# The 16-point stage of an H3 convolution: kernel spectrum without rearranged copies, five VectorE products

## The chip, the cores and the metric

The kernel runs on one core of a Trainium2 chip. The metric is device time in microseconds (us), from one launch to its end; the time before is the median of three runs. A core has a matrix engine (TensorE; in the profile PE for its matmuls and PEld for the loads of their stationary operand), a vector engine (VectorE, DVE), an engine for copies and functions (ScalarE, ACT), GpSimd (POOL) and SyncE (SP), which issues transfers. Matmuls write to PSUM, which has 8 banks of 2 KB in each of 128 partitions; everything else lies in SBUF.

## The reference

The model has four layers, A, B, A, B, on a sequence of S = 2048 rows of D = 576 channels, each one a residual around a layer norm:

```python
def _A_ref(x, ...):                     # Fourier mixing as matmuls
    a = einsum("bsd,ed->bse", x, dft_hid_re); b = einsum("bsd,ed->bse", x, dft_hid_im)
    return einsum("ts,bse->bte", dft_seq_re, a) - einsum("ts,bse->bte", dft_seq_im, b)

def _B_ref(q, k, v, shift_k, ssm_k, ssm_D):
    kv = (short causal convolution of k with shift_k) * v
    y = irfft(rfft(pad(kv)) * rfft(pad(ssm_k)))[:S]     # long causal convolution, per channel
    return q * (y + kv * ssm_D)

x = x + A(layernorm(x)); x = x + B(layernorm(x), k, v, ...)
x = x + A(layernorm(x)); x = x + B(layernorm(x), k, v, ...)
```

k, v and the two kernels are inputs, so the long convolution y is the same in both B layers and does not depend on x. It is computed once.

## The kernel before, in words

Layer A is done as two sets of float32 matmuls: the sequence transform (128x512 tiles, in four blocks of output rows, `layer` at L291) and behind it the hidden transform (`hidden`, L267, 27 matmuls of 128x288 for each of two halves of a row group). Every float32 operand is split in a rounded high part and a remainder, and each product is three matmuls (high by high, high by low, low by high). The split is one ScalarE copy and one VectorE subtraction (`split`, L90, lines L91 and L92 of the profile).

The long convolution is a Fourier transform in two factors, 128 by 16, written as a generator (`branch`, L338) that the loop over the first layer A advances piece by piece, so that its matmuls stand between those of the layer. It has three stages: 128-point products (tile f1r), then the 16-point stage (MID), then 128-point products of the inverse (i2). The loop sets the order by costs that it adds up: from its step MID_FROM = 47 to I2_END = 111 it counts what part of the layer has been issued and draws from the generator until the branch has had the same part (L746 to L754). The numbers that the generator yields are these costs.

The 16-point stage has 64 groups (mids): two halves of the channels by 32 groups of four frequencies, 288 channels wide. For each group the generator issues, in this order:

- `mid_inverse` (L515) of an earlier group: three matmuls, a ScalarE copy out of PSUM and a store;
- `mid_kernel` (L493): three matmuls give the spectrum of the convolution kernel in PSUM (pk), with real parts in partitions 0 to 63 (lo) and imaginary parts in 64 to 127 (hi). ScalarE copies pk into half 0 of an SBUF tile kk, and then makes three more copies of 64 partitions within kk, so that half 0 holds the real parts twice and half 1 the imaginary parts with the two signs that the complex product needs;
- `mid_round` (L510) of the group before: the split of its product (line L485 on ScalarE, L491 on VectorE);
- `mid_signal` (L501): three matmuls give the spectrum of the signal in PSUM (px); VectorE makes the complex product out of a product of 128 partitions (L504), two of 64 (L505 and L506) and a sum (L507). The result lies in kk's half 0;
- the split of the operand that is needed two groups later (`split_feed`, again L485 and L491, 576 wide) and the next load.

The ScalarE instructions of the stage are recorded at L485, a helper (`act`) that also chains each one behind the one before it. The matmuls are all at L74. The PSUM tiles of the stage (name bk) are taken in turn from three banks, which the hidden transform uses too; the sequence transform has five banks of its own (s and rm). A bank is free again when the copy or the last product that reads it is done.

Of the kernel before, what the change touches and what calls it, by code (L numbers as in the profile page):

```python
# [12 lines left out]
AF = mybir.ActivationFunctionType  # L13
OP = mybir.AluOpType
# [7 lines left out]
HD = D // 2  # L22
# [42 lines left out]
def fnet_h3_kernel(ctx: ExitStack, tc: tile.TileContext, x, c_mat, w_re, w_im, k_pad, v, shift_k,  # L65
                   ssm_k, ssm_d, f1c, i2c, midc, out):
    nc = tc.nc
# [68 lines left out]
    def two(v):  # L136
        return v.rearrange("p (a n) -> p a n", a=2)
# [200 lines left out]
    def branch():  # L338
# [132 lines left out]
        lo, hi = slice(0, 64), slice(64, 128)  # L471

        def mid_half(df, o):
            ps = bank()
            mm(ps[:, :HD], mc[:, 0, :], df[0][:, o:o + HD], True, False)
            mm(ps[:, :HD], mc[:, 0, :], df[1][:, o:o + HD], False, False)
            mm(ps[:, :HD], mc[:, 1, :], df[0][:, o:o + HD], False, True)
            return ps
# [3 lines left out]
        def act(*args, **kw):  # L482
            if last_act:
                with tc.issue_after(last_act[-1]):
                    last_act.append(nc.scalar.activation(*args, **kw).ins)  # L485
            else:
                last_act.append(nc.scalar.activation(*args, **kw).ins)
# [5 lines left out]
        def mid_kernel(df):  # L493
            pk, kk = mid_half(df, HD), two(ring["kk"]())
            act(kk[:, 0, :], pk[:, :HD], AF.Copy)
            act(kk[lo, 1, :], kk[hi, 0, :], AF.Copy)
            act(kk[hi, 1, :], kk[hi, 0, :], AF.Copy, scale=-1.0)
            act(kk[hi, 0, :], kk[lo, 0, :], AF.Copy)
            return kk

        def mid_signal(df, kk):  # L501
            px = mid_half(df, 0)
            p1, p2 = kk[:, 0, :], ring["p2"]()
            nc.vector.tensor_tensor(p1, px[:, :HD], p1, OP.mult)  # L504
            nc.vector.tensor_tensor(p2[lo], px[hi, :HD], kk[hi, 1, :], OP.mult)  # L505
            nc.vector.tensor_tensor(p2[hi], px[lo, :HD], kk[lo, 1, :], OP.mult)  # L506
            nc.vector.tensor_tensor(p1, p1, p2, OP.add)  # L507
            return p1

# [62 lines left out]
        for i, (kind, hf, q) in enumerate(feeds):  # L572
            df = halves.pop(i)
            if kind:
                i2_products(hf, q, fcs.pop(used), df)
                load_fc(used + ahead)
                used += 1
            else:
                if len(yfs) == MID_LAG:
                    mid_inverse(*yfs.pop(0))  # L580
                    yield 0.4
                kk = mid_kernel(df)
                if product is not None:
                    yfs.append((*product[:2], mid_round(product[2])))
                yield 1.6
                product = hf, q, mid_signal(df, kk)
# [517 lines left out]
```

## Time and profile before

| | before |
|---|---|
| time, median of three runs | 1202.64 us (1201.62 to 1203.9) |
| the profiled execution's own time | 1203.45 us |
| its span, first to last instruction | 1201.7 us |
| mean granted TensorE clock | 0.998 |
| TensorE matmuls busy | 1181.4 us (98%) |
| weight loads busy | 1026.7 us (85%) |
| VectorE busy | 839.9 us (70%) |
| ScalarE busy | 666.0 us (55%) |
| the 16-point stage's first and last product on VectorE | 222.4 and 550.0 us |

Busy time is the union of an engine's instruction records; the matmuls' ends are modelled, so that a busy TensorE may still lose time between two matmuls. In a table of stretches of time a row has the stretch and its length, then for PE, PEld, DVE, ACT and POOL the busy time with the number of instructions, then the granted clock, the share of the transfer engines and their GB/s; where it is asked for one tile or line, it has the busy time of those instructions alone. In a group of instructions stand line, engine, operation, output<-inputs, shapes and count, then busy time and the mean of one in ns, then the idle time before them. "Idle before" in a row is the idle time of that engine right before the instruction, with the instruction that ended it. In a list of waits the columns are the total, the number of waits and the longest. In a timeline they are the start, the busy time, the engine, the line, the operation, output<-inputs, the number of merged instructions, and in brackets the idle time before.

### The profile page before, as it was taken

What the parts mean: (1) busy time and instruction counts of PE and PEld (TensorE: products, weight loads), DVE (VectorE), ACT (ScalarE), POOL (GpSimd) and SP (SyncE); (2) the same over time, 40 slices, a digit from 0 to 9 for tenths busy, and PEclk for the clock granted to TensorE, in tenths of its full rate; (3) what the DMA queues carried; (4) which work ended last, traced back from release to release, by engine and by line L of the source; (5) the groups of instructions that cost most, each with busy time, mean ns of one, the idle gap of its engine ahead of it and who ended that gap; (6) DMA issues with size and microseconds to landing.
All of it is one profiled execution on the core that took longest, in us unless ns stands there. A gap on an engine that the chain in (4) does not pass through costs nothing.

```text
span 1201.7 us, 18251 instructions
## 1 busy us (share of the span) xinstructions
PE 1181.4 (98%) x6320; PEld 1026.7 (85%) x6320; DVE 839.9 (70%) x1498; ACT 666.0 (55%) x1335; POOL 75.3 (6%) x116
## 2 busy tenths in 40 slices
PE   7999999999999999999999999999999999999997
PEld 6888888988888888888988898888888888789997
DVE  7889983679777677675447766865776777674764
ACT  7865665679877768675435666534444445450210
POOL 2210000000000000001101121000000000001111
PEclk9999999999999999999999999999999999999999
DMA  9879898546756767648967686872772786795621
GB/s 355 273 242 310 282 296 262 177 133 182 217 183 194 212 178 207 194 143 247 308 202 237 221 257 204 278 259 71 225 274 71 216 283 213 270 339 155 218 92 40
DMA packets 146110, 261.95 MB, mean 218 GB/s; under 512 B 15841, under 2 KB 44769, under 8 KB 146018
## 3 DMA queue, kind: packets, MB, share of 16 engines
q1 hardware_dynamic: 102674, 205.58, 53.5%
q10 hardware_dynamic: 36432, 42.63, 10.2%
q0 software_dynamic: 6912, 12.59, 3.9%
q8 instruction: 49, 0.80, 0.3%
q14 instruction: 43, 0.35, 0.1%
HBM read 194.09 MB, written 66.65 MB: 217 GB/s over the span
## 4 chain that ended last, share of the span: by engine, by line
PE 84%; DVE 5%; ACT 4%; DMA 4%; issue 2%; POOL 1%; SPq 0%; ACTq 0%; POOLq 0%; DVEq 0%
PE s L74 46%; PE bk L74 33%; PE rm L74 5%; ACT flts L485 1%; DMA flts<-in_c_mat 1%; DVE mats L189 1%; DMA t<-ud 1%; DVE mats L92 1%; DVE f1f L386 1%; DMA t<-flts 1%; ACT mid L485 1%; ACT mats L91 1%; POOL flts L615 0%; DVE f1f L381 0%; DMA flts<-in_ssm_k 0%
## 5 line engine op out<-in xcount | busy, mean ns | idle before, releaser
L74 PE MATMUL s<-mats 128*128 128x512 f32 x2088 | 531.4, 392 | 1.3 <-DVE u L92 0.8
L74 PEld LDWEIGHTS s<-mats 128*128 128x128 f32 x2088 | 381.7, 188 | 71.9 <-DVE u L92 1.7
L92 DVE TENSOR_TENSOR mats<-flts,mats 128x512 fp32r<-128x512 f32 x206 | 141.1, 687 | 60.9 <-ACT mats L91 57.8
L91 ACT ACTIVATE mats<-flts 128x512 fp32r<-128x512 f32 x206 | 128.6, 628 | 81.8 <-PE bk L74 33.8
L74 PE MATMUL bk<-mid 128*128 128x288 f32 x768 | 131.2, 300 | 1.7 <-ACT flts L485 0.9
L74 PEld LDWEIGHTS bk<-mid 128*128 128x128 f32 x768 | 114.3, 188 | 21.3 <-ACT flts L485 8.4
L491 DVE TENSOR_TENSOR mid<-flts,mid 128x576 fp32r<-128x576 f32 (+1 forms) x160 | 101.9, 637 | 33.6 <-ACT mid L485 28.0
L74 PE MATMUL bk<-w,u 128*128 128x288 f32 x864 | 120.8, 296 | 0.4 <-DVE w L232 0.4
L74 PEld LDWEIGHTS bk<-w,u 128*128 128x128 f32 x864 | 117.3, 188 | 4.1 <-ACT flts L485 1.3
L485 ACT ACTIVATE flts<-bk 128x288 f32<-128x288 f32 x160 | 62.0, 405 | 86.8 <-PE bk L74 73.9
L74 PE MATMUL rm<-mats 128*128 128x512 f32 x304 | 94.9, 391 | 0.0
L485 ACT ACTIVATE mid<-flts 128x576 fp32r<-128x576 f32 (+1 forms) x159 | 86.7, 582 | 7.3 <-DMA flts<-t 3.3
L485 ACT ACTIVATE flts<-flts 64x288 f32<-64x288 f32 x192 | 85.0, 443 | 5.9 <-ACT flts L485 0.4
L431 ACT ACTIVATE flts<-bk 128x288 f32<-128x288 f32 x128 | 49.2, 409 | 47.1 <-PE bk L74 40.0
L74 PE MATMUL bk<-f1r 128*128 128x288 f32 x384 | 64.9, 301 | 7.2 <-ACT f1r L91 7.2
L74 PEld LDWEIGHTS bk<-f1r 128*128 128x128 f32 x384 | 59.8, 192 | 14.2 <-ACT f1r L91 7.6
L74 PE MATMUL bk<-mats 128*128 128x288 f32 (+1 forms) x376 | 67.8, 317 | 0.0
L74 PEld LDWEIGHTS rm<-mats 128*128 128x128 f32 x304 | 56.9, 188 | 12.1 <-DVE flts L264 0.3
L74 PE MATMUL s<-t,mats 128*128 128x512 f32 x264 | 65.5, 390 | 1.6 <-DVE t L92 1.6
L278 DVE TENSOR_TENSOR flts<-flts,bk 128x288 f32<-128x288 f32 x48 | 21.8, 453 | 63.2 <-PE bk L74 61.0
L175 POOL TENSOR_TENSOR flts<-flts 128x1 f32<-128x1 f32 x35 | 29.6, 846 | 526.0 <-DVE flts L174 522.6
L74 PEld LDWEIGHTS s<-t,mats 128*128 128x128 f32 x264 | 49.5, 188 | 12.2 <-DVE t L92 2.0
(143 smaller groups left out, 1500.7 us busy)
## 6 DMA issues: line engine op xcount, KB each, us to landing
flts<-in_c_mat SPq DMA_DIRECT2D x148, 256.0 KB, 3.7
ph<-in_c_mat SPq DMA_DIRECT2D x54, 512.0 KB, 4.4
t<-flts ACTq DMA_DIRECT2D x64, 288.0 KB, 4.5
flts<-t SPq DMA_DIRECT2D x64, 288.0 KB, 2.9
flts<-in_c_mat SPq DMA_DIRECT2D x30, 512.0 KB, 5.0
vd<-flts ACTq DMA_DIRECT2D x64, 144.0 KB, 2.3
flts<-vd SPq DMA_DIRECT2D x32, 288.0 KB, 4.9
mid<-in_i2c POOLq DMA_DIRECT2D x32, 256.0 KB, 5.6
```

Of the source, the lines that this page charges most:

```text
L74: nc.tensor.matmul(ps, lhsT, rhs, start=first, stop=last, skip_group_check=more)
L91: a = nc.scalar.activation(h, src, AF.Copy).ins
L92: return a, nc.vector.tensor_tensor(l, src, h.bitcast(F32), OP.subtract).ins
L175: pows.append(nc.gpsimd.tensor_tensor(rs, ve, mhalf, OP.pow).ins)
L189: made.append(nc.vector.tensor_tensor(t[:, D + REM:], y[:, :NC * P], h[:, :NC * P], OP.subtract).ins)
L278: added[:] = [nc.vector.tensor_tensor(r[:, cs], r[:, cs], ps[:, :HD], OP.add).ins]
L386: nc.vector.tensor_tensor(rp, rp, out_t, OP.add)
L431: stored[:] = [nc.scalar.activation(so[:, c, :], ps[:, :HD], AF.Copy).ins]
L485: last_act.append(nc.scalar.activation(*args, **kw).ins)
L491: nc.vector.tensor_tensor(l, src, h.bitcast(F32), OP.subtract)
```

## The change

ScalarE only copies pk into half 0 of kk. The real parts then stand in partitions 0 to 63 and the imaginary parts in 64 to 127, once. VectorE makes the complex product from that, with four products of 64 partitions instead of one of 128 and two of 64; the sign is in the first one. In two of the four (the second and the third) the operand in PSUM and the one in SBUF begin at different partitions. The result is written over kk's half 0 after the last product that reads that part. The sum is as before, so that there are five VectorE instructions for a group in the place of four.

```diff
         def mid_kernel(df):
             pk, kk = mid_half(df, HD), two(ring["kk"]())
             act(kk[:, 0, :], pk[:, :HD], AF.Copy)
-            act(kk[lo, 1, :], kk[hi, 0, :], AF.Copy)
-            act(kk[hi, 1, :], kk[hi, 0, :], AF.Copy, scale=-1.0)
-            act(kk[hi, 0, :], kk[lo, 0, :], AF.Copy)
             return kk
 
         def mid_signal(df, kk):
             px = mid_half(df, 0)
             p1, p2 = kk[:, 0, :], ring["p2"]()
-            nc.vector.tensor_tensor(p1, px[:, :HD], p1, OP.mult)
-            nc.vector.tensor_tensor(p2[lo], px[hi, :HD], kk[hi, 1, :], OP.mult)
-            nc.vector.tensor_tensor(p2[hi], px[lo, :HD], kk[lo, 1, :], OP.mult)
+            nc.vector.scalar_tensor_tensor(p2[lo], px[hi, :HD], -1.0, kk[hi, 0, :], op0=OP.mult, op1=OP.mult)
+            nc.vector.tensor_tensor(p2[hi], px[lo, :HD], kk[hi, 0, :], OP.mult)
+            nc.vector.tensor_tensor(p1[hi], px[hi, :HD], kk[lo, 0, :], OP.mult)
+            nc.vector.tensor_tensor(p1[lo], px[lo, :HD], kk[lo, 0, :], OP.mult)
             nc.vector.tensor_tensor(p1, p1, p2, OP.add)
             return p1
```

## The prediction

> **What bounds the kernel now.** I read the page first (busy shares and the chain), then the stage's stretch of time with its matmul counts, then who waits for whom there, then the timeline of single groups.
>
> ```profile
> PE 1181.4 (98%) x6320; PEld 1026.7 (85%) x6320; DVE 839.9 (70%) x1498; ACT 666.0 (55%) x1335; POOL 75.3 (6%) x116
> ...
> PE 84%; DVE 5%; ACT 4%; DMA 4%; issue 2%; POOL 1%; SPq 0%; ACTq 0%; POOLq 0%; DVEq 0%
> ```
>
> TensorE is busy for 98% of the span and makes up 84% of the chain that ended last. The change removes no matmul, so it can only win the time that TensorE loses in the 16-point stage, from about 219 to 560 us. "Busy" does not show this loss well, so I take it from counts. Two stretches without this stage give the undisturbed pace: 760 to 1040 us has only 512-wide matmuls, 1080 to 1180 us only 288-wide ones. The last row counts the 288-wide ones among the 1918 of the stage.
>
> ```profile
> 219.00:560.00 341.00, 338.92 (x1918) 295.00 (x1917) 252.65 (x496) 253.27 (x551) 7.42 (x14) 1.00 0.62 184
> 760.00:1040.00 280.00, 280.00 (x1237) 231.91 (x1236) 198.52 (x272) 125.64 (x207) 0.00 (x0) 1.00 0.63 208
> 1080.00:1180.00 100.00, 100.00 (x756) 100.00 (x755) 61.00 (x128) 12.68 (x21) 13.12 (x13) 1.00 0.46 148
> ...
> 219.00:560.00 341.00, 176.07 (x1134) 1.00 0.62 184
> ```
>
> 280 / 1237 = 0.2264 us for a 512-wide matmul, 100 / 756 = 0.1323 us for a 288-wide one. The stage has 784 and 1134 of them: 177.5 + 150.0 = 327.5 us of the 341. So TensorE loses 13.5 us here, 1.1% of the kernel: that is the ceiling. VectorE (252.65 us) and ScalarE (253.27 us) are both near 74% in this stretch. The waits of the weight loads tell what TensorE was held for:
>
> ```profile
> PEld bk L74 <- ACT flts L485: 9.5, 27, 0.8
> PEld bk L74 <- DVE flts L506: 3.0, 7, 0.9
> ```
>
> And one group in the timeline shows how such a wait comes about:
>
> ```profile
> 485.60 0.41 ACT L485 ACTIVATE flts<-bk 128x288 f32<-128x288 f32 x1 [1.36 <-PE bk L74]
> 486.05 1.37 ACT L485 ACTIVATE flts<-flts 64x288 f32<-64x288 f32 x3
> ...
> 487.92 0.46 DVE L491 TENSOR_TENSOR mid<-flts,mid 128x288 fp32r<-128x288 f32 x1 [3.18 <-ACT mid L485]
> 488.01 1.53 PE L74 MATMUL s<-mats 128*128 128x512 f32 x6
> ...
> 489.24 0.45 DVE L506 TENSOR_TENSOR flts<-bk,flts 64x288 f32<-64x288 f32 x1
> ...
> 489.74 0.43 PEld L74 LDWEIGHTS bk<-mid 128*128 128x128 f32 x3 [0.62 <-DVE flts L506]
> ```
>
> The copy of pk begins at 485.60; the three copies of 64 partitions follow for 1.37 us; only then comes the rounding, for which VectorE (L491) has waited 3.18 us; the three products stand behind that, and when the last of them, L506 at 489.24, is done the px bank is free and TensorE goes on. Six 512-wide matmuls from 488.01 would have ended at 488.01 + 6 x 0.2264 = 489.37, the next could only begin with its load at 489.74: TensorE lost 0.37 us where the load's idle time is 0.62. I use this ratio, 0.6, to turn idle time of the loads into time lost.
>
> **ScalarE loses three copies a group.**
>
> ```profile
> L485 ACT ACTIVATE flts<-flts 64x288 f32<-64x288 f32 x192 | 85.0, 443 | 5.9 <-ACT flts L485 0.4
> ```
>
> 192 copies of 443 ns, 85.0 us of ScalarE. Its load in the stage falls from 253 to 168 us of 341. What this is worth is bounded by the waits for ScalarE: 9.5 us of load idle time x 0.6 = 5.7 us. Not all of it comes from the queue on ScalarE. Part is the bare latency of a copy that ScalarE begins the moment the matmuls are done. One cycle of the pattern that repeats between 340 and 441 us has both kinds:
>
> ```profile
> 343.56 0.41 ACT L485 ACTIVATE flts<-bk 128x288 f32<-128x288 f32 x1 [0.46 <-PE bk L74]
> 344.01 1.37 ACT L485 ACTIVATE flts<-flts 64x288 f32<-64x288 f32 x3
> 344.03 0.43 PEld L74 LDWEIGHTS bk<-mid 128*128 128x128 f32 x3 [0.26 <-ACT flts L485]
> ...
> 346.77 0.43 PEld L74 LDWEIGHTS bk<-mid 128*128 128x128 f32 x3 [0.43 <-ACT flts L485]
> ...
> 350.66 0.44 PEld L74 LDWEIGHTS bk<-mid 128*128 128x128 f32 x3 [0.33 <-ACT flts L485]
> ```
>
> At 343.56 ScalarE itself was idle and waiting for TensorE, so the 0.26 us stays. The 0.43 and 0.33 us come behind the copies of 344.01 and go. That is 0.76 of 1.02, three quarters: 5.7 x 0.75 = 4.3 us. The stall at 489.74 is booked under L506 but has the same cause (VectorE had waited 3.18 us for ScalarE), another 0.4 us. Gain: 4.7 us. Bounds: nothing, if every wait is latency, and 5.7 + 3.0 x 0.6 = 7.5 us, if all waits for ScalarE and L506 go. What is late next where a stall goes is VectorE.
>
> **VectorE gets one instruction more.**
>
> ```profile
> L505 DVE TENSOR_TENSOR flts<-bk,flts 64x288 f32<-64x288 f32 x64 | 29.4, 459 | 1.7
> L504 DVE TENSOR_TENSOR flts<-bk,flts 128x288 f32<-128x288 f32 x64 | 29.1, 455 | 37.1 <-ACT flts L485 36.6
> ...
> L92 DVE TENSOR_TENSOR w<-flts,w 128x576 fp32r<-128x576 f32 x4 | 3.0, 758 | 7.3 <-ACT w L91 7.3
> L232 DVE SCALAR_TENSOR_TENSOR w<-flts,w 128x576 fp32r<-128x576 f32 x4 | 3.0, 757 | 5.8 <-ACT w L231 5.8
> ```
>
> A product of 64 partitions takes as long as one of 128 (459 against 455 ns), so splitting L504 in two saves nothing. The instruction with the factor -1.0 costs what a plain product costs (757 against 758 ns at L232 and L92). So four products for three.
>
> Two of them have their operands at different partitions, which no row shows. The low end is no extra cost, not a gain: L505, which writes 64 partitions away from where it reads, is 4 ns over L504. The high end is a second pass, 2 x 0.46 us a group. I take the low end, because L505 is the nearest row.
>
> One after the other, products start 0.47 us apart (below, 287.25 to 287.72). So 64 x 0.47 = 30 us more on VectorE. In most of the stage that is covered by its idle time: L504 alone has waited 36.6 us for ScalarE, waits that go. The cover is missing where VectorE has hardly any idle time:
>
> ```profile
> 273.00:300.00 27.00, 26.59 (x142) 22.99 (x142) 25.12 (x52) 24.85 (x58) 0.00 (x0) 1.00 0.65 191
> ...
> 326.00:340.00 14.00, 13.57 (x73) 11.53 (x72) 12.63 (x24) 11.78 (x24) 0.00 (x0) 1.00 0.65 208
> ...
> 441.00:460.00 19.00, 18.83 (x94) 15.29 (x93) 16.83 (x33) 16.18 (x35) 1.06 (x2) 1.00 0.61 174
> ```
> ```profile
> DVE flts L504 <- ACT flts L485: 0.8, 1, 0.8
> DVE mats L92 <- ACT mats L91: 0.3, 1, 0.3
> ```
> ```profile
> 286.75 0.46 DVE L491 TENSOR_TENSOR mid<-flts,mid 128x288 fp32r<-128x288 f32 x1
> 287.25 0.46 DVE L505 TENSOR_TENSOR flts<-bk,flts 64x288 f32<-64x288 f32 x1
> 287.72 0.45 DVE L506 TENSOR_TENSOR flts<-bk,flts 64x288 f32<-64x288 f32 x1
> 288.20 0.76 DVE L491 TENSOR_TENSOR mid<-flts,mid 128x576 fp32r<-128x576 f32 x1
> 288.88 0.45 DVE L507 TENSOR_TENSOR flts<-flts 128x288 f32<-128x288 f32 x1
> ```
> ```profile
> 273.00:340.00 67.00, 6.85 (x15) 1.00 0.66 199
> 273.00:300.00 27.00, 3.19 (x7) 1.00 0.65 191
> 326.00:340.00 14.00, 0.91 (x2) 1.00 0.65 208
> 441.00:460.00 19.00, 1.34 (x3) 1.00 0.61 174
> ```
>
> From 273 to 300 us VectorE is busy 25.12 of 27 us, and of the 1.88 idle only 0.8 + 0.3 = 1.1 are waits (the second fence lists them all); the rest is the small gaps seen in the third. Seven groups fall in it (the last fence counts L504 by stretches). They need 7 x 0.47 = 3.3 us more; 1.1 can be used, so VectorE is 2.2 us short. It works for TensorE in a fixed order with three banks, so TensorE pays: 2.2 us lost. Bounds: nothing, if the lag is carried into the slacker time after 300 us; 3.3 us, if the waits stay. From 326 to 340 us, 2 groups, 12.63 + 0.9 is under 14; from 441 to 460 us, 3 groups, 16.83 + 1.4 is under 19: both fit, barely, and cost nothing while no wait falls in between.
>
> A rule to weigh here: by the Trainium skill, "VectorE: DVE Perf Modes", section on two Vector instructions with no wait between them, an instruction whose input or output begins in another quadrant than its predecessor's waits until that one has ended, and one that does not starts earlier. The trace agrees: the 0.76 us L491 at 288.20 is followed after 0.68 us, L505 by L506 only after 0.47. By that rule all four new products are held, each by the one before, while L504, which begins at the same partitions as the subtractions of 128 ahead of it, can now start 0.08 us early; 7 x 0.08 = 0.6 us more would make the loss 2.8 and the sum -1.9 us.
>
> **What else moves.** Half 1 of kk is unused, no tile gets smaller. No transfer, queue or POOL instruction is added, moved or passed. The first product now waits for one ScalarE copy instead of four; behind it on VectorE stand the rest of the group and the split of the next operand, for which TensorE waits two groups later. The px bank is released by the fourth product instead of the third, 0.47 us later where VectorE sets the pace, earlier where ScalarE did (1.37 - 0.47 = 0.9 us).
>
> **Sum.** -4.7 + 2.2 = -2.5 us. Against the profiled execution's 1203.45 us that is 1200.95; this execution lies 0.8 us over the median of the three runs, 1202.64, so I say 1200.1 us. About 0.2% (2.4 us) is what a measurement of this kernel can tell from no change.
>
> **Rivals.** First, little is won: the waits for ScalarE are mostly latency and stay. For it speaks that 32 of the copies out of PSUM began with ScalarE idle:
>
> ```profile
> ACT flts L485 <- PE bk L74: 51.6, 32, 3.8
> ```
>
> Against it, the 0.43 and 0.33 us above stand behind a queue. With half the gain (2.3 us) and the same loss the time is 1202.5, no change.
>
> Second, slower: VectorE becomes the bound not only in the seven groups but wherever it waits for something that does not come earlier, so that its lag is never made up before 340 us. Then the block's end at 326 to 340 us counts too. 15 groups from 273 to 340 us x 0.47 = 7.1 us, less the 1.1 us of waits, 6.0 lost, against a gain of no more than 2: 1206.6 us. It decides when VectorE needs over 0.3 us a group more than TensorE gives it. The Trainium skill, same page, "Rules for kernel authors", says to keep the number of VectorE instructions low; by it this rival is the likely one. No run here shows it yet.
>
> Third, a second pass for the two mixed products: 64 x 0.92 = 59 us more, 252.65 + 30 + 59 = 342 us of 341. VectorE would be the bound in the whole stage, over 10 us slower. Nothing in the rows points to it.
>
> **Chances.** The forecast 0.53 (own range 1196.0 to 1202.5: from a gain of 6.6 us and no loss to a gain of 2.3 and a loss of 2.2), of it 0.40 under -2.4 us and 0.13 within. Little won 0.18, within. VectorE the bound 0.25, slower. Second pass 0.04, slower. So faster 0.40, same 0.31, slower 0.29. The range reaches from 1196.0 to 1206.8 and leaves out the second pass and some of the forecast's best end.
>
> **What would show it.** Right: 192 rows fewer at 64x288 on ScalarE, its busy time 581 us; VectorE's busy time near 869 us, 0.46 us for each product; waits of the loads for L485 down from 9.5 to about 2.5 us; waits for the last product up; 273 to 300 us stretched by about 2 us. Wrong: products over 0.5 us; waits for ScalarE unchanged; stalls on VectorE in other stretches, since the order of instructions on each engine is drawn up anew for the changed program; a difference outside 219 to 560 us.

## The result and the profile after

The changed kernel takes 1208.32 us (median of 6 runs, 1207.23 to 1209.49); the kernel before took 1203.27 us beside it (6 runs, 1201.62 to 1205.88). The ratio is 1.0041, 95% interval 1.0029 to 1.0052: slower by 0.41%, about 5 us, where 2.5 us of gain were forecast. The profiled execution took 1208.35 us with a span of 1206.6 us, at a clock of 0.999.

From the page of the changed kernel, the busy times and the chain that ended last:

```profile
PE 1182.0 (98%) x6320; PEld 1026.1 (85%) x6320; DVE 874.4 (72%) x1562; ACT 579.3 (48%) x1143; POOL 75.8 (6%) x116
...
PE 76%; DVE 12%; DMA 5%; ACT 3%; issue 2%; POOL 0%; SPq 0%; ACTq 0%; POOLq 0%; DVEq 0%
```

ScalarE has lost its 192 copies (666.0 to 579.3 us). VectorE has 64 instructions and 34.5 us more, and its share of the chain has gone from 5% to 12%, while TensorE's fell from 84% to 76%. The products themselves, grouped by line and shape over the stage, cost what was forecast; L501 is the one with the factor -1.0, L502 and L503 are the two whose operands stand at different partitions:

```profile
L503 DVE TENSOR_TENSOR flts<-bk,flts 64x288 f32<-64x288 f32 x64 | 29.5, 461 | 2.0
L501 DVE SCALAR_TENSOR_TENSOR flts<-bk,flts 64x288 f32<-64x288 f32 x64 | 29.4, 459 | 13.8 <-ACT flts L485 9.3 <-PE bk L74 0.8
L502 DVE TENSOR_TENSOR flts<-bk,flts 64x288 f32<-64x288 f32 x64 | 28.8, 451 | 1.1
...
L504 DVE TENSOR_TENSOR flts<-bk,flts 64x288 f32<-64x288 f32 x64 | 28.7, 449 | 1.9
```

Where the time went is read from stretches of time, with all matmuls first and those of the small tiles (bk) alone in the second fence. For before, 262 to 345 us:

```profile
262.00:345.00 83.00, 82.15 (x435) 70.20 (x434) 68.05 (x133) 68.44 (x148) 0.00 (x0) 1.00 0.63 186
```
```profile
262.00:345.00 83.00, 31.47 (x189) 1.00 0.63 186
```

For after, the same:

```profile
262.00:345.00 83.00, 79.55 (x398) 64.16 (x397) 74.84 (x145) 44.18 (x93) 0.00 (x0) 1.00 0.59 176
```
```profile
262.00:345.00 83.00, 28.32 (x159) 1.00 0.59 176
```

At the prediction's paces (0.2264 us for a 512-wide matmul, 0.1323 for a 288-wide one) before does 246 x 0.2264 + 189 x 0.1323 = 80.7 us of work in these 83 us and loses 2.3. After does 239 and 159 of them, 75.1 us, and loses 7.9. That is 5.6 us more, all of the 5. Counted the same way, 219 to 262 us went from 2.1 to 1.2 us lost and 345 to 570 us from 8.4 to 9.6: taken together, these two stretches show nothing of the gain that was forecast for ScalarE's copies.

One group of the worst place shows how. The timeline of after; of TensorE and the weight loads only the matmuls of the px tile are shown:

```profile
309.91 0.63 PE L74 MATMUL bk<-mid 128*128 128x288 f32 x3 [0.26 <-DVE flts L504]
...
310.63 0.46 DVE L501 SCALAR_TENSOR_TENSOR flts<-bk,flts 64x288 f32<-64x288 f32 x1 [0.38 <-PE bk L74]
311.12 0.46 DVE L491 TENSOR_TENSOR mid<-flts,mid 128x288 fp32r<-128x288 f32 x1
...
311.61 0.45 DVE L502 TENSOR_TENSOR flts<-bk,flts 64x288 f32<-64x288 f32 x1
...
312.09 0.76 DVE L491 TENSOR_TENSOR mid<-flts,mid 128x576 fp32r<-128x576 f32 x1
...
312.88 0.46 DVE L503 TENSOR_TENSOR flts<-bk,flts 64x288 f32<-64x288 f32 x1
...
313.37 0.69 DVE L92 TENSOR_TENSOR mats<-flts,mats 128x512 fp32r<-128x512 f32 x1
...
314.10 0.45 DVE L504 TENSOR_TENSOR flts<-bk,flts 64x288 f32<-64x288 f32 x1
314.58 0.46 DVE L505 TENSOR_TENSOR flts<-flts 128x288 f32<-128x288 f32 x1
...
314.69 0.63 PE L74 MATMUL bk<-mid 128*128 128x288 f32 x3 [0.35 <-DVE flts L504]
```
```profile
315.42 0.46 DVE L501 SCALAR_TENSOR_TENSOR flts<-bk,flts 64x288 f32<-64x288 f32 x1 [0.38 <-PE bk L74]
```

The same place before:

```profile
307.29 0.46 DVE L504 TENSOR_TENSOR flts<-bk,flts 128x288 f32<-128x288 f32 x1 [1.23 <-ACT flts L485]
307.75 0.46 DVE L491 TENSOR_TENSOR mid<-flts,mid 128x288 fp32r<-128x288 f32 x1
308.25 0.46 DVE L505 TENSOR_TENSOR flts<-bk,flts 64x288 f32<-64x288 f32 x1
308.72 0.45 DVE L506 TENSOR_TENSOR flts<-bk,flts 64x288 f32<-64x288 f32 x1
309.20 0.76 DVE L491 TENSOR_TENSOR mid<-flts,mid 128x576 fp32r<-128x576 f32 x1
...
311.65 0.46 DVE L504 TENSOR_TENSOR flts<-bk,flts 128x288 f32<-128x288 f32 x1 [0.72 <-ACT flts L485]
```

Before, the first and the last product are 307.29 and 308.72: one small split stands between the products, the px bank is held for 1.88 us, and the big splits come after. After, three splits stand *between* the four products, L491 twice and the layer's L92: the bank is held from 310.63 to 314.55, 3.92 us. (This is one of the worst groups. Added up from the timelines over all 64 groups, the bank is held for 112 us before and 202 after, 1.75 and 3.15 a group, and 8 groups pass 3.5 us.) TensorE begins the next px at 314.69, just behind the fourth product, and VectorE begins the next first product at 315.42, just behind that px. Each waits for the other, and a group takes 4.79 us (310.63 to 315.42) where it took 4.36 (307.29 to 311.65). VectorE itself needs 4.79 - 0.38 = 4.41 us for a group; before it needed 4.36 - 0.72 = 3.64.

Over the whole stage (219 to 570 us) the weight loads and matmuls of after had these waits. The loads' wait for ScalarE was 9.7 us before. For the last product matmuls waited 0.6 us before and loads 3.0 (for L506); after, it is matmuls alone. The largest wait of the loads is new, none is listed before: the profile calls it "issue" and names no releaser. At 309.88 and 314.66 such a load (0.65 and 0.75 us idle) belongs to the px matmuls that wait for the fourth product above.

```profile
PEld bk L74 <- issue: 8.3, 14, 1.6
PEld bk L74 <- ACT flts L485: 6.0, 22, 0.9
```
```profile
PE bk L74 <- DVE flts L504: 3.8, 10, 1.2
```

### The profile page after: what moved, and what is told of

Same layout as the page of the kernel before. It is cut to its first block, busy times and chain, and to the rows that moved or that the text cites. A ratio compares the mean times of both kernels' runs of the same rounds, so it can differ in the third digit from the quotient of the medians.

```text
span 1206.6 us, 18178 instructions
## 1 busy us (share of the span) xinstructions
PE 1182.0 (98%) x6320; PEld 1026.1 (85%) x6320; DVE 874.4 (72%) x1562; ACT 579.3 (48%) x1143; POOL 75.8 (6%) x116
## 4 chain that ended last, share of the span: by engine, by line
PE 76%; DVE 12%; DMA 5%; ACT 3%; issue 2%; POOL 0%; SPq 0%; ACTq 0%; POOLq 0%; DVEq 0%
PE s L74 42%; PE bk L74 30%; PE rm L74 4%; DVE mid L491 2%; DVE mats L92 2%; DMA flts<-in_c_mat 1%; ACT mid L485 1%; DMA t<-ud 1%; DVE flts L504 1%; DMA flts<-t 1%; DVE flts L503 1%; DVE flts L505 1%; ACT mats L91 1%; DVE flts L502 1%; DVE u L92 1%
## 5 line engine op out<-in xcount | busy, mean ns | idle before, releaser
L92 DVE TENSOR_TENSOR mats<-flts,mats 128x512 fp32r<-128x512 f32 x206 | 140.9, 686 | 52.3 <-ACT mats L91 47.7
L491 DVE TENSOR_TENSOR mid<-flts,mid 128x576 fp32r<-128x576 f32 (+1 forms) x160 | 101.8, 638 | 36.7 <-ACT mid L485 31.2
L485 ACT ACTIVATE mid<-flts 128x576 fp32r<-128x576 f32 (+1 forms) x159 | 86.7, 581 | 76.6 <-DVE flts L505 65.3
L485 ACT ACTIVATE flts<-bk 128x288 f32<-128x288 f32 x160 | 63.4, 407 | 96.3 <-PE bk L74 79.3
L74 PE MATMUL bk<-mats,t 128*128 128x288 f32 (+1 forms) x368 | 59.3, 303 | 0.0
L74 PEld LDWEIGHTS bk<-mats 128*128 128x128 f32 x376 | 55.6, 188 | 3.4
```

The source lines that it names most:

```text
L74: nc.tensor.matmul(ps, lhsT, rhs, start=first, stop=last, skip_group_check=more)
L92: return a, nc.vector.tensor_tensor(l, src, h.bitcast(F32), OP.subtract).ins
L491: nc.vector.tensor_tensor(l, src, h.bitcast(F32), OP.subtract)
```

## The experiments

The theory after the first look: the five instructions are not too much work; it is their place among VectorE's other work that costs. In the source each group's products stand together, and the split of the next operand behind them. But the order on each engine is drawn up anew when the program is compiled, and it is held only where an edge demands it. The result overwrites half 0 of kk, which the products read, so the third and the fourth must wait for the earlier ones, and the compiler put other work in between. The rival is the prediction's second: one product more a group is too much for VectorE, wherever it stands. The effects below are ratio - 1, times 1203.3 us.

### The same work, order pinned (e1)

```diff
-        with behind(*stored):
+        with behind(*stored, *product_end):
             halved[:] = split(t[0], t[1], raw)
...
-            nc.vector.tensor_tensor(l, src, h.bitcast(F32), OP.subtract)
+            with behind(*product_end):
+                low_end[:] = [nc.vector.tensor_tensor(l, src, h.bitcast(F32), OP.subtract).ins]
...
+            with behind(*low_end):
+                i = nc.vector.scalar_tensor_tensor(p2[lo], px[hi, :HD], -1.0, kk[hi, 0, :], op0=OP.mult, op1=OP.mult).ins
+            for o, x, k in ((p2[hi], lo, hi), (p1[hi], hi, lo), (p1[lo], lo, lo)):
+                with tc.issue_after(i):
+                    i = nc.vector.tensor_tensor(o, px[x, :HD], kk[k, 0, :], OP.mult).ins
+            product_end[:] = [i]
```

Each first product waits for the last split that the stage has issued, the four follow each other, and the next splits, the layer's (L92) among them, wait for the fourth.

> The changed kernel with the order on VectorE pinned: the rounding of the group before, then the four products directly one behind the other, then the splits of the next operands. No instruction is added or taken away. Theory BANK (the four products were drawn up between the splits, so that the px bank is held 3 to 4 us and the next group's matmuls wait for it): the hold falls to about 1.9 us, most of the loss goes, 1203 to 1205 us. Theory LOAD (VectorE simply has one instruction a group more than the stretch has time for, wherever it stands): 1207 to 1209 us, as the changed kernel.

Measured: 1200.41 us, ratio 0.9973 (0.9962 to 0.9983), -3.2 us. The same instructions in another order are 8.2 us faster than the changed kernel (the ratios differ by 0.0068), faster than the kernel before, and faster than either theory had it. The order of TensorE's matmuls was drawn up anew with it; that part was not held fixed. Busy times of the pinned form:

```profile
PE 1177.0 (98%) x6320; PEld 1026.0 (86%) x6320; DVE 863.8 (72%) x1562; ACT 578.7 (48%) x1143; POOL 75.1 (6%) x116
```

The same 1562 instructions keep VectorE busy for 863.8 us instead of 874.4. In this form the products overwrite as in the changed kernel, so the overwriting itself costs the hardware nothing that is seen here.

### The two sides of the sum, one at a time (e2, e3)

The kernel before without its three copies, and with three products of the same sizes that need no copy. It leaves out the sign and reads the wrong halves, so it doesn't compute the convolution. Against the kernel before:

```diff
-            act(kk[lo, 1, :], kk[hi, 0, :], AF.Copy)
-            act(kk[hi, 1, :], kk[hi, 0, :], AF.Copy, scale=-1.0)
-            act(kk[hi, 0, :], kk[lo, 0, :], AF.Copy)
...
+            nc.vector.tensor_tensor(p2[lo], px[hi, :HD], kk[hi, 0, :], OP.mult)
+            nc.vector.tensor_tensor(p2[hi], px[lo, :HD], kk[lo, 0, :], OP.mult)
             nc.vector.tensor_tensor(p1, px[:, :HD], p1, OP.mult)
-            nc.vector.tensor_tensor(p2[lo], px[hi, :HD], kk[hi, 1, :], OP.mult)
-            nc.vector.tensor_tensor(p2[hi], px[lo, :HD], kk[lo, 1, :], OP.mult)
```

So it is not ScalarE's part alone: the product of 128 partitions, the first before, is now the last of the three.

> The kernel before with the three ScalarE copies of a group left out and its three products kept (they read half 0 of kk as it is; the complex product is left out of the computation in that its factors are the wrong halves). This is the ScalarE part of the change alone. The prediction's term: 4.7 us won, 1198.6 us. If the waits for ScalarE were only latency: 1203 us.

Measured: 1197.34 us, ratio 0.9954 (0.9941 to 0.9968), -5.5 us. The forecast's -4.7 lies inside. The loads' waits for ScalarE did not fall to 2.5 us but to 4.5:

```profile
PEld bk L74 <- ACT flts L485: 4.5, 17, 1.0
```

The other side: the copies kept, the 128-partition product cut in two.

```diff
-            nc.vector.tensor_tensor(p1, px[:, :HD], p1, OP.mult)
+            nc.vector.tensor_tensor(p1[lo], px[lo, :HD], p1[lo], OP.mult)
+            nc.vector.tensor_tensor(p1[hi], px[hi, :HD], p1[hi], OP.mult)
```

> The kernel before, all copies kept, with its product of 128 partitions cut in two of 64. This is the extra VectorE instruction alone. The prediction's term: 2.2 us lost, 1205.5 us. Theory LOAD: about the loss of the whole change plus the gain it hid, 1208 to 1213 us. Theory BANK: between 1205 and 1208, by where the fourth product is put.

Measured: 1207.56 us, ratio 1.0039 (1.0026 to 1.0051), +4.7 us (3.1 to 6.1), over twice the forecast's 2.2. The order was drawn up anew here too, but no long hold came of it: in no group does the bank stay held for more than 2.38 us. So with the copies kept, one product more can cost this much without the splits between the products. The sum of the two, -5.5 + 4.7 = -0.8, is not the +4.9 of the change, so at least one more term is in it.

### The pins alone, on the kernel before (e4)

The same edges as in e1 on the three products and the splits of the kernel before.

> Control: the kernel before with the same order pinned (rounding, three products in a row, then the splits). Theory BANK: the hold before was already short (1.8 us from the first product to the end of the last), 1202 to 1204 us. Theory LOAD: 1203 us, no change. If it moves by more than 2 us, pinning does something of its own and the run with the changed kernel must be read against this one.

Measured: 1212.54 us, ratio 1.0073 (1.006 to 1.0086), +8.8 us. Both theories had it near 1203. So the pins are no gift in themselves, and e1's gain isn't theirs alone. With the copies still there, the chain on ScalarE delays the rounding, and every product is now pinned behind it. VectorE's largest wait in the stage:

```profile
DVE mid L493 <- ACT mid L486: 72.4, 57, 3.2
```

Before, the wait of that kind was 14.1 us. A pinned order is as good as the slowest thing pinned ahead.

### No overwriting, no pins (e5)

```diff
-            p1, p2 = kk[:, 0, :], ring["p2"]()
+            p1, p2 = kk[:, 1, :], ring["p2"]()
```

The result goes to the unused half 1 of kk. Nothing else is changed.

> The changed kernel with one edit: the third and fourth product and the sum write into half 1 of kk, which is free, in place of half 0, over which the changed kernel writes while earlier products read it. The order on VectorE is not pinned. In its program the four products now stand next to each other. Theory OVERWRITE (the writes over half 0 made the planner put other work between the products, and so held the px bank): as with the pinned order or better, 1198 to 1201 us. Theory LOAD: 1207 to 1209 us. If only the pins of the first experiment helped, by something else than the products standing together: 1203 to 1208 us.

Measured: 1200.89 us (12 runs), ratio 0.9973 (0.996 to 0.9986), -3.2 us, the same as e1 with one index changed. The profiled execution is 3 us over this median, and what it lost lies ahead of the stage. One group in its timeline:

```profile
312.20 0.46 DVE L491 TENSOR_TENSOR mid<-flts,mid 128x288 fp32r<-128x288 f32 x1 [0.51 <-ACT mid L485]
312.67 0.46 DVE L501 SCALAR_TENSOR_TENSOR flts<-bk,flts 64x288 f32<-64x288 f32 x1
313.14 0.45 DVE L502 TENSOR_TENSOR flts<-bk,flts 64x288 f32<-64x288 f32 x1
313.61 0.46 DVE L503 TENSOR_TENSOR flts<-bk,flts 64x288 f32<-64x288 f32 x1
314.08 0.45 DVE L504 TENSOR_TENSOR flts<-bk,flts 64x288 f32<-64x288 f32 x1
314.46 0.74 DVE L491 TENSOR_TENSOR mid<-flts,mid 128x576 fp32r<-128x576 f32 x1
315.12 0.45 DVE L505 TENSOR_TENSOR flts<-flts 128x288 f32<-128x288 f32 x1
315.49 0.68 DVE L92 TENSOR_TENSOR mats<-flts,mats 128x512 fp32r<-128x512 f32 x1
316.46 0.46 DVE L491 TENSOR_TENSOR mid<-flts,mid 128x288 fp32r<-128x288 f32 x1 [0.29 <-ACT mid L485]
317.04 0.46 DVE L501 SCALAR_TENSOR_TENSOR flts<-bk,flts 64x288 f32<-64x288 f32 x1
```

The four products stand together (312.67 to 314.53, 1.86 us of the bank), and the splits behind them. A group takes 4.37 us (312.67 to 317.04), as before. And VectorE needs only 4.26 - 0.29 = 3.97 us from one L491 of 288 to the next (312.20 to 316.46), against 4.41 for the same eight instructions after. Two things are gained by standing together, then: the bank comes free 2 us sooner, and VectorE saves 0.44 us a group. The second is seen in the starts. L491 begins 0.38 us after L504 (314.08 to 314.46), L92 0.37 us after the sum (315.12 to 315.49), each before its predecessor has ended. After, every one of the eight begins only behind the end of the one ahead.

By the Trainium skill, "VectorE: DVE Perf Modes", section on two Vector instructions with no wait between them, an instruction is held until all earlier ones have finished if an input begins in another quadrant (32 partitions) than the first input of the last instruction that read that memory, or its output in another than the last one written there. The rows agree, even where it is not obvious. L504 follows L92 only after 0.73 us (313.37 to 314.10), although both begin at partition 0: its PSUM operand is to be compared with that of L503, which begins at 64. By this rule, products of 64 partitions mixed with splits of 128 are held at each change; in e5's order there are fewer changes. The sum of after (314.58) would not be held by it; it reads what L504 has just written.

### The sum moved to GpSimd (e6)

e5 with one line more, to give VectorE back its 64 instructions:

```diff
-            nc.vector.tensor_tensor(p1, p1, p2, OP.add)
+            nc.gpsimd.tensor_tensor(p1, p1, p2, OP.add)
```

> As the run with half 1, and the sum of the two products on GpSimd in place of VectorE, so that VectorE has four instructions a group, as before the change. If what is left of the loss is VectorE's load between 273 and 345 us: 2 to 3 us under the run with half 1, 1196 to 1198 us. If the rounding behind the sum is on the path and GpSimd is slower than 0.45 us at it: no gain, or a loss of 1 to 3 us.

Measured: 1214.62 us, ratio 1.0092 (1.0078 to 1.0107), +11.1 us, 13.7 over e5, where 1 to 3 us was the largest loss expected. The group on GpSimd, and ScalarE's wait for it:

```profile
L505 POOL TENSOR_TENSOR flts<-flts 128x288 f32<-128x288 f32 x64 | 96.2, 1503 | 242.5 <-DVE flts L504 215.6 <-ACT mats L91 16.2 <-ACT mid L485 3.9
```
```profile
ACT mid L485 <- POOL flts L505: 73.1, 43, 3.2
```

A sum takes 1503 ns there and 450 on VectorE, and ScalarE, whose next instruction rounds it, waits. Relieving VectorE's queue gained nothing that shows; the latency of the path cost far more.

### Two copies and three products (e7, e9)

In between: ScalarE copies the real parts into both parts of half 1, VectorE makes the two mixed products of 64 from half 0 and one product of 128 in half 1. Against the changed kernel:

```diff
+            act(kk[hi, 1, :], kk[lo, 0, :], AF.Copy)
+            act(kk[lo, 1, :], kk[lo, 0, :], AF.Copy)
...
+            p1, p2 = kk[:, 1, :], ring["p2"]()
-            nc.vector.tensor_tensor(p1[hi], px[hi, :HD], kk[lo, 0, :], OP.mult)
-            nc.vector.tensor_tensor(p1[lo], px[lo, :HD], kk[lo, 0, :], OP.mult)
+            nc.vector.tensor_tensor(p1, px[:, :HD], p1, OP.mult)
```

> Half way: ScalarE makes two copies of 64 partitions (the real parts twice into half 1), VectorE has three products, one of 128 partitions with both operands at partition 0, and the sign in the first; the sum goes into half 1. One ScalarE copy less than before the change, no VectorE instruction more. A third of the gain of leaving out all three copies (6.3 us): about 1201.5 us. If one instruction more on VectorE is what costs, and the copies cost little: under the run with half 1.

Measured: 1196.29 us, ratio 0.9938 (0.9924 to 0.9953), -7.5 us: the fastest of all, faster than both kernels and 5 us under its forecast. The other forecast came true, that it would be under e5: with one product fewer and two copies more than e5 it is 4.3 us faster. That speaks for a cost of the added instruction even where the products stand together, though the two also differ in their order. From 262 to 345 us, all matmuls, then those of bk:

```profile
262.00:345.00 83.00, 82.90 (x439) 70.95 (x439) 69.20 (x139) 59.88 (x133) 0.00 (x0) 1.00 0.63 194
```
```profile
262.00:345.00 83.00, 31.49 (x189) 1.00 0.63 194
```

250 x 0.2264 + 189 x 0.1323 = 81.6 us of work: 1.4 us lost. To see what the copy saved is worth, e9 makes the second copy twice, so that ScalarE has as many copies as before:

```diff
+            act(kk[lo, 1, :], kk[lo, 0, :], AF.Copy)
```

> The run with two copies and three products (1196.3 us), with the second copy made twice, so that ScalarE has as many instructions as before the change. If its gain comes from the ScalarE copy saved: back to 1202 to 1204 us. If it comes from the products standing together without an overwrite: 1197 to 1198 us.

Measured: 1197.32 us, ratio 0.9957 (0.9945 to 0.9968), -5.2 us. With three copies and as many products as before it still gains. And the loads wait much less for ScalarE (9.7 us before), with all 192 copies there:

```profile
PEld bk L74 <- ACT flts L485: 2.7, 14, 0.2
```

The copy is worth 1.0 us by the medians and 2.3 by the ratios, whose intervals overlap; the rest comes with the new arrangement, in which the first two products need none of these copies and nothing that a copy or a later product reads is overwritten. Which of the two does more was not taken apart. It also puts e2 in another light: most of what was gained there can be had without leaving out a copy.

### How much of it is the bank (e8)

e5, but the third and the fourth product are issued and pinned behind the split of the next operand, so that the bank is held nearly as long as in the changed kernel without any overwriting:

```diff
+            def rest():
+                with behind(*low_end):
                     nc.vector.tensor_tensor(p1[hi], px[hi, :HD], kk[lo, 0, :], OP.mult)
                     nc.vector.tensor_tensor(p1[lo], px[lo, :HD], kk[lo, 0, :], OP.mult)
                 nc.vector.tensor_tensor(p1, p1, p2, OP.add)
...
             split_feed(i + 2)
+            while late_half:
+                late_half.pop()()
```

> The run with half 1 again (nothing overwritten, 1200.9 us), but with the third and fourth product issued and pinned behind the split of the next operand, as they stood in the changed kernel. Same instructions, same tiles, only these two later. Theory BANK (what costs is how long the products hold the px bank): the time goes back up to 1205 to 1209 us and the loads wait for the fourth product again. If the overwriting itself was slow, by something else than the order: it stays at 1200 to 1202 us.

Measured: 1201.19 us (11 runs), ratio 0.9987 (0.9978 to 0.9996), -1.6 us: only 1.7 us worse than e5. The forecast of the theory of the bank, 1205 us at least, fell. Over the stage e8 holds the bank for 188 us against 131 in e5 and 202 after, so the length of the hold alone does not set the time. A group of its timeline (L507 is the fourth product here):

```profile
309.35 0.46 DVE L501 SCALAR_TENSOR_TENSOR flts<-bk,flts 64x288 f32<-64x288 f32 x1
...
312.04 0.45 DVE L507 TENSOR_TENSOR flts<-bk,flts 64x288 f32<-64x288 f32 x1
312.41 0.67 DVE L92 TENSOR_TENSOR mats<-flts,mats 128x512 fp32r<-128x512 f32 x1
```

The hold is long, 309.35 to 312.49, but it is 3.14 us and not 3.92: L92 stands behind the fourth product. The next guess was that a hold of 3.1 us leaves TensorE time for the next px, and one of 3.9 doesn't (the closed loop).

### The layer's split in and out of the hold (e10, e11)

Two kernels take that up. e10 is the changed kernel with one edge more, which keeps L92 behind the fourth product; e11 is e1 without that edge.

```diff
-        with behind(*stored):
+        with behind(*stored, *product_end):      # e10 adds it to the changed kernel, e11 takes it from e1
             halved[:] = split(t[0], t[1], raw)
```

> The changed kernel with one instruction moved in part of the groups: the split of the layer's matrix (L92, 0.67 us) may not begin before the fourth product of the group, as it does between the third and the fourth in the changed kernel from about 300 to 345 us and again later. The split of the next operand (0.76 us) stays between the second and the third product, so the px bank is still held for about 3.1 us a group, but no longer for 3.9. CLOSED LOOP (the hold costs only where it and the next px matmuls, 0.86 us, together pass the 4.4 us that TensorE's own work of a group takes; 3.9 + 0.86 passes it, 3.1 + 0.86 does not): most of the loss goes, 1201 to 1204 us. IN PROPORTION (every microsecond of hold costs alike): the hold falls by about a tenth of its sum, 1207 us or more. OVERWRITE ITSELF (the third and fourth product are slow to start because they write what others read): no change, 1208 us.

> The pinned form of the changed kernel (four products ahead of the splits of the 16-point stage), without the pin on the split of the layer's matrix (L92), which then falls between the products in about a third of the groups, once or twice in a group: the px bank is held 1.9 us plus 0.7 or 1.4 us there. CLOSED LOOP: no hold passes 3.5 us, nothing is lost, 1200 to 1202 us as with the pin. IN PROPORTION: about 20 us of hold more than with the pin, where 90 us more cost 7.4: 1202 us. The run mainly tells whether the L92 split between products harms by itself, in which case 1204 us or more.

Measured: e10 1204.59 us, ratio 1.0019 (1.0008 to 1.003), +2.3 us; e11 1202.08 us, ratio 1.0006 (0.9995 to 1.0016), +0.7 us (their kernel before ran at 1202.19). One split moved out of the hold gives back 2.6 of the 8.2 us; the same split moved in costs 4.0 by the ratios. So the place of L92 is a real part of the loss. But no theory is borne out. Beside a kernel before of 1203.3 us, as in the other runs, the ratios give 1205.6 us for e10 and 1204.0 for e11. e10 lies between the closed loop's 1201 to 1204 us and the 1207 or more of the theory in proportion, and e11 should have lost nothing against e1; it stands where its forecast had the split harm by itself. Against the proportion speaks that 11 us of hold less (191 against 202) gave 2.6 us, while e8, with 188, is 3.9 faster than e10. That the overwriting itself is slow, e1 has already ruled out.

A group of e11 shows what L92 inside the hold does (L507 are the second to fourth product, L509 is the sum, L493 the split):

```profile
302.57 0.69 DVE L92 TENSOR_TENSOR mats<-flts,mats 128x512 fp32r<-128x512 f32 x1
303.29 0.45 DVE L507 TENSOR_TENSOR flts<-bk,flts 64x288 f32<-64x288 f32 x1
...
304.33 0.45 DVE L509 TENSOR_TENSOR flts<-flts 128x288 f32<-128x288 f32 x1
305.29 0.46 DVE L493 TENSOR_TENSOR mid<-flts,mid 128x288 fp32r<-128x288 f32 x1 [0.51 <-ACT mid L486]
```

And of e1, in the same place:

```profile
303.45 0.44 DVE L509 TENSOR_TENSOR flts<-flts 128x288 f32<-128x288 f32 x1
303.82 0.68 DVE L92 TENSOR_TENSOR mats<-flts,mats 128x512 fp32r<-128x512 f32 x1
304.43 0.44 DVE L493 TENSOR_TENSOR mid<-flts,mid 128x288 fp32r<-128x288 f32 x1
```

In e11 the sum is followed at once by the subtraction that needs ScalarE's rounding of this very sum: 0.51 us idle. In e1 L92 stands between them and covers this latency. From 296 to 329 us e11 takes 4.66 us for each group, e1 3.94 us for the three from 301 us on and at most 4.39 for the next three. Read from these timelines, and not tested, the latency of the rounding has become part of the loop that sets e11's pace there. The same 0.51 us stands in some groups of e10 too, but e8 has it in as many (4 of these waits from 262 to 345 us in each): it doesn't explain why e10 is slower than e8.

The table sets the kernels with the five instructions side by side: time lost by TensorE in three stretches, counted as above, VectorE's busy time from the page, the time that the px bank is held (first product's start to last product's end, over 64 groups), and the effect on the time.

| kernel | 219 to 262 | 262 to 345 | 345 to 570 | sum, us | VectorE busy, us | bank held, us | effect, us |
|---|---|---|---|---|---|---|---|
| before (four instructions) | 2.1 | 2.3 | 8.4 | 12.8 | 839.9 | 112 | |
| after | 1.2 | 7.9 | 9.6 | 18.7 | 874.4 | 202 | +4.9 |
| e10, L92 out of the hold | 1.2 | 6.4 | 8.8 | 16.4 | 871.6 | 191 | +2.3 |
| e11, pinned, L92 free | 1.7 | 6.5 | 6.0 | 14.2 | 867.2 | 144 | +0.7 |
| e8, late third and fourth | 2.3 | 4.5 | 5.5 | 12.3 | 870.4 | 188 | -1.6 |
| e5, half 1 | 2.4 | 4.2 | 5.9 | 12.5 | 866.5 | 131 | -3.2 |
| e1, pinned | 1.0 | 4.1 | 6.5 | 11.6 | 863.8 | 126 | -3.2 |

The same five instructions span 8 us by their order. The lost time follows the effect only to within some 3 us: e5's sum is 0.3 us under before where the time is 3.2 under, and for e1 it is 1.2; each row is one execution, and what lies outside these stretches isn't counted. What stays open: e8 and e10 have nearly the same order on VectorE from 300 to 345 us and nearly the same hold, but e10 loses 1.9 us more than e8 from 262 to 345 us and 3.3 us more after that. TensorE's own order also differs between any two of these programs, and that wasn't isolated.

## Why the prediction was wrong

It said 1200.1 us, in a range of 1196.0 to 1206.8; 1208.3 lies outside, on the other side of no change.

- **The view of the bound held.** TensorE's lost time in the stage explains the result of the change to within a microsecond (12.8 to 18.7 us, against +4.9 measured).
- **ScalarE's three copies: the size fits, the reason is not shown.** Forecast 4.7 us of gain, measured 5.5 (3.8 to 7.1) in e2, which also puts the products in another order. The busy time, 579.3 us, is the 581 forecast. But the loads' waits for L485 fell only to 4.5 us in e2 and 6.0 in the changed kernel, not to 2.5, while e9, with all three copies, gets them down to 2.7 and gains 5.2 us. So the load on ScalarE is not what counted most; more likely it is what the prediction lists under "What else moves" without a price, that the first product no longer waits for the copies. The ratio of 0.6 was read from one stall as well: at 344.03, 346.77 and 350.66, with 1, 9 and 7 512-wide matmuls from 343.70, 344.53 and 348.99 ahead of them, TensorE lost 0.10, 0.20 and 0.10 us of 1.02 idle, a ratio of 0.4, by which 4.7 would have been about 3. That the forecast came so near e2 is partly luck.
- **The products held.** 449 to 461 ns each, no second pass for mixed partitions; the third rival is out.
- **The extra product on VectorE held as a term where the products stand together.** Forecast 2.2 us of loss; e1 and e5 against e2, -3.2 against -5.5, give 2.3. In other surroundings it is more: e3 gives 4.7, and e5 is 4.3 us slower than e7, which has one product fewer and two copies more. The whole sum of -2.5 is within the interval of e1 and e5, which run these instructions (e5 with another place for the result). In the changed kernel's own order it did not: VectorE's need of a group at 310 us rose by 0.77 us (3.64 to 4.41), not by 0.47, since each of its eight instructions begins only behind the end of the one ahead. The rule of held instructions had been weighed, but for the products alone (0.6 us), not for the splits mixed in, and by comparing each instruction with the one ahead of it only.
- **The step that failed:** "The px bank is released by the fourth product instead of the third, 0.47 us later where VectorE sets the pace". It took the order of before for granted. The compiled program puts up to three splits between the products, and at 310 us the bank is held 3.92 us instead of 1.88: 2.04 us later, not 0.47 (1.4 us on the mean of 64 groups). With e1 and e5 the order is shown to be the term that was missing: +8.2 us between the same instructions in two orders, and what set the order is the overwriting, since one index undoes it. How the 8.2 us divide between the bank, VectorE's held instructions, the rounding behind the sum and TensorE's own new order stays open. The longer hold alone does not account for them: e8 holds the bank for 188 us of the 202 and is 6.5 us faster by the ratios. e10 puts 2.6 us on the one split.
- **The second rival** came near the time (1206.6) and named the place (273 to 340 us), but not the cause. It blames one more instruction a group, 15 x 0.47 us; e1 and e5 have that instruction and are faster than before. That it came so near is luck. The stretch from 300 to 326 us, which the prediction had called slacker, is among the worst: 137 matmuls before, 120 after (rows of after and before below, in this order).

```profile
300.00:326.00 26.00, 24.30 (x120) 19.21 (x119) 22.94 (x46) 13.14 (x27) 0.00 (x0) 1.00 0.69 203
```
```profile
300.00:326.00 26.00, 26.00 (x137) 22.58 (x137) 20.48 (x41) 22.32 (x48) 0.00 (x0) 1.00 0.68 203
```

The prediction did name "the order of instructions on each engine is drawn up anew" among the things that could make it wrong, and gave it no price and no chance.

## What to carry to other kernels

Where a compiler draws up each engine's order, a change of data dependence is a change of order: a result written in place has to wait for whatever still reads that place, and other work can slip in between, here 8 us for the same instructions. Write into a free buffer, or keep the few instructions that hold a scarce bank together with explicit edges; then look at the new timeline for what the moved work had been covering (in e1 the layer's split hides ScalarE's rounding, in e11 it doesn't). And price an added instruction together with the ones it lands between, not by its own duration.

## What the runs showed of the hardware

- A product of 64 partitions whose PSUM and SBUF operands stand 64 partitions apart takes 451 or 461 ns, as long as one with both at the same partitions (449 or 459 ns).
- The same eight VectorE instructions take 3.97 us in a group of e5, where they stand by shape, and 4.41 in a group of after, where shapes alternate; over the kernel VectorE is busy for 866.5 us (863.8 in e1) against 874.4.
- A sum of two 128x288 f32 tiles took 1503 ns on GpSimd (e6), 450 on VectorE (after).
